# Attention, Fourier mixing and an MLP: the last batch's q and k in natural order, and the last row tile's second matrix in two halves

## The chip, the cores and the metric

The kernel runs on one core of one Trainium2 chip. The metric is the device time of one launch in microseconds (us), lower is better. Five engines work from queues of their own: TensorE (PE in the profile, with its weight loads as PEld), VectorE (DVE), ScalarE (ACT), GpSimd (POOL), and SyncE (SP), which here only issues transfers.

## The reference, cut to what matters

```python
# q, k, v: (4, 8, 768, 64); mem_k, mem_v: (4, 8, 8, 64)
for c in range(768 // 32):                    # chunks of 32 queries
    k_full = concat(mem_k, k[16 left of the chunk : 8 right of it])
    v_full = concat(mem_v, v[the same rows])
    out[chunk] = softmax(q[chunk] @ k_full.T / 8) @ v_full
x = out with the heads side by side           # (4, 768, 512)
u = x + real(fft(fft(x, axis=1), axis=2))
un = (u - mean(u)) / sqrt(var(u) + 1e-6)
y = u + relu(un @ w_ch1) @ w_ch2              # 512 -> 2048 -> 512
```

## The kernel before, in words

There are four batches (b = 0 to 3), and each goes through three stages: attention, a Fourier transform by matrices, and the MLP. Attention works on pairs of heads, four pairs to a batch, numbered n = 0 to 15; a pair fills the 128 partitions with 2 x 64 head dimensions. For each pair, q and k are loaded (`e_load_qk`, cast to bf16 by the GpSimd queue), turned so that the head dimension lies on the partitions, and k is spread into twelve windows of 128 columns, `kTb`: 32 zeros, 8 memory keys, and 88 keys (16 left, 64 own, 8 right) for every 64 queries (`e_kT`). Then come two groups (g = 0, 1) of scores (`e_scores`, 12 matmuls of 64 columns each), the exponential on ACT (`e_exp`), the values (`e_values`, 24 matmuls) and the division (`e_norm`, DVE).

A load puts 8 rows of q or k side by side on one partition (row = 8 p + j, RB = 8), so the turned matrix has its columns in the order j, then p. In batches 0 to 2 TensorE turns them (`turn`), and the copies out of PSUM (`e_qT`, `e_kT`, line 415) put the columns back in natural order. In batch 3 (`b >= TURNED`) a transposing DMA on SP does the turning (`e_flip_q`, `e_flip_k`), and the order stays interleaved: `e_kT` (line 410, on ACT) gathers each window with a stride of 128 columns, and `e_scores` reads q in runs of 8 and writes its 64 scores with a stride of 8, so that they come out in natural order. `kU`, the turned k of batch 3 with a margin of zeros, is cleared once at the start by GpSimd (line 851).

The MLP takes three row tiles at a time (sh = 0, 1). `e_ch1` (line 741) makes 16 blocks of 128 hidden units by 384 rows, 4 matmuls each; `e_relu` (ACT, line 749) moves each to SBUF; then for each row tile `e_ch2` (line 756) adds 16 matmuls of 512 columns in one PSUM bank, `e_osb` (DVE, line 763) multiplies by the row's scale and adds u, and a store follows. Four PSUM banks serve the MLP and the Fourier stage (`acc0`, `acc1`, `mlp0`, `mlp1`). In batches 1 to 3 row tiles 3 to 5 are stored in two hops (lines 771 and 778: the Fourier stage leaves their rows mirrored); the others in one (`e_out`, line 768). The order of the row tiles in these batches is 0, 3, 4, 5, 1, 2, so the last tile of all is 2, stored in one hop from ACT's queue.

The order on every engine is fixed beforehand by `Plan.order`, a scheduler in Python: each task (`add`) has an engine, a cost in us, what it comes after, and the buffers that it takes and gives back. On every engine the first task in rank order that can start by the plan's clock is put next. MLP matmuls have a very high rank number (`MLPS`) and are marked `filler=True`: they fill whatever TensorE time the earlier stages leave. The costs that the plan uses are estimates; the chip then executes each engine's list in order, whatever the times turn out to be.

Of the kernel before, what the change touches and what calls it, by code (L numbers as in the profile page):

```python
# [177 lines left out]
def kernel(  # L178
# [54 lines left out]
        assert False  # L233

    NS = 3
    qs = [spool.tile([QP, 2, RB * D], BF16, name=f"qs{i}") for i in range(NS)]
    ks = [spool.tile([KP, 2, RB * D], BF16, name=f"ks{i}") for i in range(NS)]
    NV = 4
    va = [spool.tile([P, 2, NT, 66], FP32, name=f"va{i}") for i in range(NV)]
    NKT = 2  # L240
    KR, KS, NKU = 16, 128, 2
    kU = [spool.tile([P, RB, KS], BF16, name=f"kU{i}") for i in range(NKU)]
    kTb = [spool.tile([P, NT, P], BF16, name=f"kTb{i}") for i in range(NKT)]

    TURNED = 3
# [92 lines left out]
    def e_load_qk(n, i):  # L338
        b, pr = seq[n]
        src, dst = ((q, qs), (k, ks))[i]  # L340
        if b >= TURNED:
            for hh in range(2):
                nc.gpsimd.dma_start(
                    dst[n % NS][0:QP].rearrange("p h (j d) -> p (h j) d", d=D)[:, hh::2],
                    src[b, 2 * pr + hh].rearrange("(p j) d -> p j d", j=RB))
            return
        nc.gpsimd.dma_start(dst[n % NS][0:QP],  # L347
                            src[b, 2 * pr:2 * pr + 2].rearrange("h (p j) d -> p h (j d)", j=RB))
# [21 lines left out]
    def turn(out_, src, eye):  # L370
        w = eye.shape[1]
        for j in range(RB):
            for hh in range(2):
                nc.tensor.transpose(out_[64 * hh:64 * hh + 64, j * w:(j + 1) * w],  # L374
                                    src[:, hh, j * D:(j + 1) * D], eye)

    def e_flip_q(n):
        qT_of[n] = qT = apool.tile([P, RB, QP], BF16, tag="qT", bufs=2, name="qT")
        nc.sync.dma_start_transpose(qT, qs[n % NS].rearrange("p h c -> p (h c)"))

    def e_flip_k(n):
        nc.sync.dma_start_transpose(kU[n % NKU][:, :, KR:KR + QP],
                                    ks[n % NS][0:QP].rearrange("p h c -> p (h c)"))

    def e_turn_q(n):
        tr_of[n] = trq = aps.tile([P, S], BF16, tag="tr", bufs=1, name="trq")
        turn(trq, qs[n % NS], ident_b[0:QP, 0:QP])

    def e_qT(n):
        qT_of[n] = qT = apool.tile([P, S], BF16, tag="qT", bufs=2, name="qT")  # L390
# [3 lines left out]
    def e_turn_k(n):  # L394
        if n < HP:
            trk = bank("acc", [P, RB * KP], BF16, "trk")
        else:
            trk = aps.tile([P, RB * KP], BF16, tag="tr", bufs=1, name="trk")
        tr_of[n, 1] = trk
        turn(trk, ks[n % NS], turn_b)  # L400

    def e_mkT(n):
        b, pr = seq[n]
# [3 lines left out]

    def e_kT(n, eng=None):
        if n >= TURNED * HP:
            nc.scalar.copy(  # L410
                strided(kTb[n % NKT], MEM0 + NMEM, [[P, NT], [RB, 11], [1, RB]]),
                strided(kU[n % NKU], KR - KOFF, [[64 // RB, NT], [1, 11], [KS, RB]]))
            return
        trk = tr_of.pop((n, 1))
        (eng or nc.scalar.copy)(
            strided(kTb[n % NKT], MEM0 + NMEM, [[P, NT], [RB, 11], [1, RB]]),
            strided(trk, 0, [[64 // RB, NT], [1, 11], [KP, RB]]))
        if n < HP:
            let_go(trk)

    def e_scores(n, g):
        qT, kT = qT_of[n], kTb[n % NKT]
        sc_of[n, g] = sc = aps.tile([P, 2, 8, 64], FP32, tag="sc", bufs=1, name="sc")
        for t6 in range(6):
            t = 6 * g + t6
            for hh in range(2):
                r0 = 64 * hh
                if n < TURNED * HP:
                    own, to = qT[r0:r0 + 64, ts(t, 64)], sc[:, hh, t6, :]
                else:  # L430
                    own = strided(qT[r0:r0 + 64], t * 64 // RB, [[QP, RB], [1, 64 // RB]])
                    to = strided(sc[:, hh, t6, :], 0, [[1, RB], [RB, 64 // RB]])
                nc.tensor.matmul(to, kT[r0:r0 + 64, t, :], own, start=True, stop=True,  # L433
                                 tile_position=(r0, 0))

    def e_exp(n, g):
# [291 lines left out]
    def slot(b, i):  # L728
        return SLOT[i] if b else i
# [22 lines left out]
    def e_ch2(b, sh, stl, part):  # L752
        if part == 0:
            pc_of[b, sh, stl] = bank(pick(b, sh, stl, 0)["tag"], [P, DM], FP32, "pc")
        for ht in range(4 * part, 4 * part + 4):
            nc.tensor.matmul(pc_of[b, sh, stl], hT_of[b, sh][:, ht, ts(stl, P)], w2_sb[:, ht, :],  # L756
                             start=(ht == 0), stop=(ht == NHT - 1))

    def e_osb(b, sh, stl):
        st = slot(b, sh * 3 + stl)  # L760
        osb_of[b, st] = osb = fpool.tile([P, DM], FP32, tag="osb", bufs=4, name="osb")
        pc = pc_of.pop((b, sh, stl))
        nc.vector.scalar_tensor_tensor(osb, pc, rstd_of[b][:, st:st + 1], xs[b][:, st, :],  # L763
                                       ALU.mult, ALU.add)
        let_go(pc)
# [87 lines left out]
    def attention(n):  # L853
        nonlocal t_gate
        b, pr = seq[n]
        first = b == 0
        lq, lk = [add("POOL", 1.6 if b >= TURNED else 0.9, lambda i=i: e_load_qk(n, i),
                      take=(("qs", "ks")[i],), moved=3.1 if b >= TURNED else 1.2, grain=0.032 if b >= TURNED else 0.1, late=LATE if b else 0.0,
                      behind=t_gate if n == HP else t_xr[b - 2] if n == TURNED * HP else t_ck.get(n - 1),
                      rank={0: -4 + i, 1: -1.2 + 0.1 * i, 2: 10 + 0.1 * i}.get(n)) for i in range(2)]  # L860
        lv = add("SP", 2.5, lambda: e_load_v(n), [t_ones[n] if n < NV else None],
                 behind=t_x2.get(b - 2),
                 take=("va",), moved=2.6, grain=0.031, head=0.4, late=(0.0, 4.0, LATE, LATE)[b])
        t_lv[n] = lv
        t_ck[n] = lk
        if n == HP - 1:
            def e_gate():
                nc.gpsimd.tensor_copy(gate[64:65], va[n % NV][64:65, 1, NT - 1, 0:1])

            t_gate = add("POOL", 0.1, e_gate, [lv])  # L870
        mk = t_mk[n] = add("DVE", 0.2, lambda: e_mkT(n), [t_mkT, t_kTz[n % NKT], t_mk.get(n - 1)],
                           take=("kTb",))
        if b >= TURNED:
            eq = add("SP", 1.2, lambda: e_flip_q(n), [lq], take=("qT",), give=("qs",),
                     late=5.0, loose=True, behind=t_flip[0])
            t_flip[0] = tk = add("SP", 1.2, lambda: e_flip_k(n), [lk, t_uz], take=("kU",),
                                 give=("ks",), late=5.0, loose=True, behind=eq)
            ek = add("ACT", 2.05, lambda: e_kT(n), [tk, mk], give=("kU",))
        else:
            tq = add("PE", 0.40, lambda: e_turn_q(n), [lq, t_idb], take=("tr",), give=("qs",))  # L880
            dve = ("DVE", nc.vector.tensor_copy) if n < HP else ("ACT", None)
            eq = add("ACT", 0.80, lambda: e_qT(n), [tq], take=("qT",), give=("tr",),
                     rank=SINES - 0.5 if n == 0 else None)
            ktag = "acc" if first else "tr"
            tk = add("PE", 0.43, lambda: e_turn_k(n), [lk, t_idb, t_kz if n == 0 else t_kzs],
                     take=(ktag,), give=("ks",))
            ek = add(dve[0], 1.25 if dve[1] else 1.04, lambda: e_kT(n, dve[1]), [tk, mk],
                     give=(ktag,))
        for g in range(2):
            s_ = add("PE", 0.32, lambda g=g: e_scores(n, g), [eq, ek], take=("sc",),  # L890
                     give=("qT", "kTb") if g == 1 else ())
            t_sc[n, g] = s_
            t_exp[n, g] = x_ = add("ACT", 1.12, lambda g=g: e_exp(n, g),
                     [s_, t_masks, t_after.get(n)], take=("e1",), give=("sc",))
            tag = "mlp" if first and g == 1 else "xa"
            v_ = add("PE", 0.85, lambda g=g: e_values(n, g), [x_, lv, t_low[n % NV]], take=(tag,),
                     rank=len(plan.tasks) + (50 if (n, g) == (2, 1) else 25) if first else None,
                     give=("e1", "va") if g == 1 else ("e1",))
            take = ("xsb",) if g == 0 and n % HP == 0 else ()
            t_norm[n, g] = add("DVE", 0.78, lambda g=g: e_norm(n, g),  # L900
                               [v_, t_norm[n - n % HP, 0] if (n % HP, g) != (0, 0) else None],
                               take=take,
                               give=(tag,))
        return x_
# [198 lines left out]
    def mlp(b, t_un, rs):  # L1103
        for sh in range(2):
# [10 lines left out]
                                rank=RELU(len(plan.tasks))))  # L1115
            for stl in range(3):
                st, end_b = slot(b, 3 * sh + stl), 3 * sh + stl == NST - 1
                for part in range(4):
                    end = part == 3
                    c2 = add("PE", 0.88, lambda sh=sh, stl=stl, part=part: e_ch2(b, sh, stl, part),  # L1120
# [68 lines left out]
```

The softmax here doesn't subtract the row's maximum and nothing guards it: scores larger than these inputs give would overflow.

## Time and profile before

The time is 290.89 us (290.84 to 291.22, 3 runs); the profiled execution spans 289.2 us, at a granted TensorE clock of 0.999.

| | PE | PEld | DVE | ACT | POOL |
|---|---|---|---|---|---|
| busy, us | 272.9 | 170.5 | 166.0 | 167.7 | 65.1 |
| share of the span | 94% | 59% | 57% | 58% | 23% |

| group | count | mean ns |
|---|---|---|
| first matrix, 128x384 (L741) | 512 | 326 |
| second matrix, 128x512 (L756) | 384 | 380 |
| sum and scale of one row tile, DVE (L763) | 24 | 751 |
| scores (L433) | 384 | 205 |
| spread of k, ACT, batch 3 (L410) | 4 | 2059 |
| spread of k, ACT, batches 1 and 2 (L415) | 8 | 1038 |

Matmuls overlap in the pipeline, so a mean duration is not the time that one takes from its neighbour; that is read from the starts, and the chain of waits gives it. The chain is followed back from the last instruction: at each step to what released it. The windows give the busy time of each engine in a stretch of the span.

### The profile page before, as it was taken

To read this page: it belongs to the slowest core of one execution; us is meant where nothing else is said; L and a number is where in the kernel's file an instruction comes from. 1 tells how busy PE (TensorE), PEld (TensorE's weight loads), DVE (VectorE), ACT (ScalarE), POOL (GpSimd) and SP (SyncE) were. 2 spreads that over 40 slices of the span, in tenths; PEclk is the share of its full clock that TensorE was granted. 3 is DMA by queue.
4 is the path that set the end of the run, shared out by engine and by line. 5 is a ranking of instruction groups with operands and counts; after the bars stand their busy time and mean duration, and the time that the engine had idled before them with its cause. 6 is when DMAs were issued, how large, how long until landed. Compare 5 with 4: busy or idle time off the path is not lost.

```text
span 289.2 us, 7127 instructions
## 1 busy us (share of the span) xinstructions
PE 272.9 (94%) x2932; PEld 170.5 (59%) x2932; DVE 166.0 (57%) x345; ACT 167.7 (58%) x290; POOL 65.1 (23%) x115
## 2 busy tenths in 40 slices
PE   1588989999999999999999999999999999999994
PEld 1466678866665767556676656556654544645641
DVE  7967998862239876958675984985672012012011
ACT  6887446688777587836796466526660721712700
POOL 8844893330210172441001002010020000000000
PEclk9999999999999999999999999999999999999999
DMA  6998989999999999999797047784142504004204
GB/s 110 198 174 150 199 159 206 199 201 195 198 190 257 130 223 166 138 152 220 177 173 176 27 111 145 175 141 159 20 89 85 100 9 125 14 36 105 42 36 109
DMA packets 115968, 39.92 MB, mean 138 GB/s; under 512 B 104544, under 2 KB 111200, under 8 KB 115936
## 3 DMA queue, kind: packets, MB, share of 16 engines
q1 hardware_dynamic: 93744, 23.41, 44.8%
q0 software_dynamic: 21472, 15.21, 32.5%
q10 hardware_dynamic: 720, 0.85, 0.9%
q8 instruction: 23, 0.38, 0.5%
q14 instruction: 9, 0.07, 0.1%
HBM read 37.36 MB, written 13.37 MB: 175 GB/s over the span
## 4 chain that ended last, share of the span: by engine, by line
PE 85%; DVE 6%; POOL 5%; DMA 2%; issue 2%; ACT 0%; POOLq 0%
PE pc L756 29%; PE ph L741 29%; PE xa L456 7%; PE ps L528 5%; PE pm L679 5%; PE sc L433 3%; DMA ks<-in_k_dram 2%; PE trk L374 1%; DVE ff L615 1%; PE trq L374 1%; POOL qs L347 1%; DVE hl L635 1%; DVE up L545 1%; DVE xsb L467 1%; PE pm L579 1%
## 5 line engine op out<-in xcount | busy, mean ns | idle before, releaser
L749 ACT ACTIVATE hT<-ph 128x384 f16<-128x384 f32 x128 | 61.9, 491 | 50.6 <-PE ph L741 49.8
L741 PE MATMUL ph<-unT,w_sb 128*128 128x384 f16 x512 | 88.1, 326 | 0.0
L756 PE MATMUL pc<-w_sb,hT 128*128 128x512 f16 x384 | 87.8, 380 | 0.0
L741 PEld LDWEIGHTS <-w_sb 128*128 128x128 f16 x512 | 48.6, 98 | 32.0 <-issue 0.4
L756 PEld LDWEIGHTS <-hT 128*128 128x128 f16 x384 | 35.9, 98 | 41.0 <-issue 0.4
L763 DVE SCALAR_TENSOR_TENSOR osb<-pc,rstd,xsb 128x512 f32<-128x512 f32 x24 | 18.0, 751 | 69.3 <-PE pc L756 64.8
L440 ACT ACTIVATE e<-sc,mbias 128x384 f32<-128x384 f32 x64 | 33.6, 577 | 18.8 <-PE sc L433 18.8
L456 PEld LDWEIGHTS xa<-va,e 128*64 128x64 f32 x672 | 21.9, 137 | 7.2 <-issue 6.2
L456 PE MATMUL xa<-va,e 128*64 128x65 f32 x672 | 25.8, 226 | 0.0
L699 ACT ACTIVATE un<-xsb,mu_s 128x512 f16<-128x512 f32 x24 | 16.9, 719 | 6.6 <-DVE mu_s L694 6.6
L540 ACT CAST up<-ps 128x386 f16<-128x386 f32 x16 | 9.6, 602 | 13.8 <-PE ps L528 11.6
L693 DVE BATCH_NORM_STATS2 st<-xsb 128x6 f32<-128x512 f32 x24 | 16.6, 691 | 0.7
L467 DVE TENSOR_TENSOR xsb<-xa,zs 128x384 f32<-128x384 f32 x28 | 15.6, 558 | 1.0
L466 DVE RECIPROCAL zs<-xa 128x6 f32<-128x6 f32 x28 | 5.3, 190 | 18.1 <-PE xa L456 17.7
L518 DVE TENSOR_TENSOR lo<-ff,hi 128x768 f16<-128x768 f32 x12 | 11.4, 954 | 4.7 <-ACT hi L513 4.7
L545 DVE TENSOR_TENSOR up<-ps,up 128x386 f16<-128x386 f32 x16 | 9.5, 596 | 6.9 <-ACT up L540 6.7
L433 PE MATMUL sc<-qT,kTb 64*128 64x64 bf16 x384 | 12.6, 205 | 0.5 <-ACT e L440 0.5
L433 PEld LDWEIGHTS <-kTb 64*128 64x128 bf16 x384 | 8.5, 100 | 7.3 <-issue 6.1
L571 POOL DMA_DIRECT2D xr<-x_back x3 | 2.3, 778 | 44.3 <-DMA x_back<-x_rows 44.3
L513 ACT CAST hi<-ff 128x768 f16<-128x768 f32 x12 | 9.9, 827 | 3.3 <-DVE ff L505 3.0
L374 PE MATMUL trq<-ident_b,qs 96*64 96x96 bf16 x192 | 7.0, 220 | 5.1 <-DMA qs<-in_q_dram 5.1
L685 DVE TENSOR_TENSOR xsb<-pm,xsb 128x512 f32<-128x512 f32 x15 | 10.0, 672 | 3.2 <-PE pm L679 3.2
(150 smaller groups left out, 356.9 us busy)
## 6 DMA issues: line engine op xcount, KB each, us to landing
va<-in_v_dram SPq DMA_DIRECT2D x32, 220.0 KB
w_sb<-in_moe_w_ch_dram POOLq DMA_DIRECT2D x8, 512.0 KB, 15.1
out_dram<-osb SPq DMA_DIRECT2D x12, 256.0 KB
qs<-in_q_dram POOLq DMA_DIRECT2D x12, 192.0 KB, 6.2
ks<-in_k_dram POOLq DMA_DIRECT2D x12, 192.0 KB, 6.9
x_rows<-xsb POOLq DMA_DIRECT2D x3, 768.0 KB, 5.1
xr<-x_back POOLq DMA_DIRECT2D x3, 768.0 KB, 6.5
out_rows<-osb SPq DMA_DIRECT2D x9, 256.0 KB
```

The costliest lines, as they stand in the source:

```text
L433: nc.tensor.matmul(to, kT[r0:r0 + 64, t, :], own, start=True, stop=True, tile_position=(r0, 0))
L440: nc.scalar.activation(e1[:, :, :, ts(half, 32)], sc[:, :, 0:6, ts(half, 32)], AFT.Exp, bias=mbias[:, half:half + 1], scale=1.0 / math.sqr ...
L456: nc.tensor.matmul(xa[64 * half:64 * half + 64, st, hh, 0:65], e1[:, hh, t6, :], v1[:, hh, 6 * g + t6, 0:65], start=True, stop=True)
L467: nc.vector.tensor_tensor(xs[b][:, 3 * g:3 * g + 3, 2 * pr * D:(2 * pr + 2) * D] .rearrange("p s (h d) -> p s h d", h=2), xa[:, :, :, 0:D] ...
L528: nc.tensor.matmul(out_[:, sp, :], part[:, ab, sp * 3 + st, c0:c1], tab[:, sp, st, :], start=(st == 0 and i == 0), stop=(st == 2 and i == 1))
L679: nc.tensor.matmul(pm[:, par, :], lhs, rhs[:, par, :], start=(im == 0), stop=(im == 3))
L693: nc.vector.bn_stats(st6, xs[b][:, kt, :])
L699: nc.scalar.activation(un, xs[b][:, kt, :], AFT.Identity, bias=mu_of[b][:, kt, 0:1], scale=-1.0)
L741: nc.tensor.matmul(ph[:, 0:384], w1_sb[:, dt, ts(ht, P)], unT_of[b][:, dt, sh * 384:(sh + 1) * 384], start=(dt == 0), stop=(dt == NDT - 1))
L749: nc.scalar.activation(hT_of[b, sh][:, ht, :], ph[:, 0:384], AFT.Relu, bias=0.0, scale=-1.0)
L756: nc.tensor.matmul(pc_of[b, sh, stl], hT_of[b, sh][:, ht, ts(stl, P)], w2_sb[:, ht, :], start=(ht == 0), stop=(ht == NHT - 1))
L763: nc.vector.scalar_tensor_tensor(osb, pc, rstd_of[b][:, st:st + 1], xs[b][:, st, :], ALU.mult, ALU.add)
```

## The change

It has two parts. In batch 3 the loads put row p of each block of 128 on partition p, so that the transposing DMA leaves q and k in natural order. Scores then read and write runs of 64 as in the other batches, and the spread of k copies runs of 88 keys, which is given to DVE in place of ACT. `kU` shrinks from 1024 to 800 columns. In the last row tile of the last batch the second matrix is done as two halves of 256 columns, each with its own PSUM bank, its own sum on DVE and its own store (the first from SP, the second from ACT), so that the work after the last matmul is half as large.

```diff
-    qs = [spool.tile([QP, 2, RB * D], BF16, name=f"qs{i}") for i in range(NS)]
-    ks = [spool.tile([KP, 2, RB * D], BF16, name=f"ks{i}") for i in range(NS)]
+    qs = [spool.tile([P, 2, RB * D], BF16, name=f"qs{i}") for i in range(NS)]
+    ks = [spool.tile([P, 2, RB * D], BF16, name=f"ks{i}") for i in range(NS)]
...
-    KR, KS, NKU = 16, 128, 2
-    kU = [spool.tile([P, RB, KS], BF16, name=f"kU{i}") for i in range(NKU)]
+    KR, NKU = 16, 2
+    kU = [spool.tile([P, KR + S + KR], BF16, name=f"kU{i}") for i in range(NKU)]
...
-                    dst[n % NS][0:QP].rearrange("p h (j d) -> p (h j) d", d=D)[:, hh::2],
-                    src[b, 2 * pr + hh].rearrange("(p j) d -> p j d", j=RB))
+                    strided(dst[n % NS], hh * D, [[2 * D, NST], [1, D]]),
+                    src[b, 2 * pr + hh].rearrange("(a p) d -> p a d", p=P))
...
-        nc.sync.dma_start_transpose(qT, qs[n % NS].rearrange("p h c -> p (h c)"))
+        nc.sync.dma_start_transpose(qT.rearrange("p (a s) -> p a s", s=P),
+                                    qs[n % NS].rearrange("p h c -> p (h c)")[:, 0:S])
...
-        nc.sync.dma_start_transpose(kU[n % NKU][:, :, KR:KR + QP],
-                                    ks[n % NS][0:QP].rearrange("p h c -> p (h c)"))
+        nc.sync.dma_start_transpose(kU[n % NKU][:, KR:KR + S].rearrange("p (a s) -> p a s", s=P),
+                                    ks[n % NS].rearrange("p h c -> p (h c)")[:, 0:S])
...
         if n >= TURNED * HP:
-            nc.scalar.copy(
-                strided(kTb[n % NKT], MEM0 + NMEM, [[P, NT], [RB, 11], [1, RB]]),
-                strided(kU[n % NKU], KR - KOFF, [[64 // RB, NT], [1, 11], [KS, RB]]))
+            win = LEFT + 64 + RIGHT
+            nc.vector.tensor_copy(
+                strided(kTb[n % NKT], MEM0 + NMEM, [[P, NT], [1, win]]),
+                strided(kU[n % NKU], KR - LEFT, [[64, NT], [1, win]]))
...
-                if n < TURNED * HP:
-                    own, to = qT[r0:r0 + 64, ts(t, 64)], sc[:, hh, t6, :]
-                else:
-                    own = strided(qT[r0:r0 + 64], t * 64 // RB, [[QP, RB], [1, 64 // RB]])
-                    to = strided(sc[:, hh, t6, :], 0, [[1, RB], [RB, 64 // RB]])
-                nc.tensor.matmul(to, kT[r0:r0 + 64, t, :], own, start=True, stop=True,
+                nc.tensor.matmul(sc[:, hh, t6, :], kT[r0:r0 + 64, t, :],
+                                 qT[r0:r0 + 64, ts(t, 64)], start=True, stop=True,
                                  tile_position=(r0, 0))
...
+    def e_ch2_half(b, sh, stl, half):
+        pc_of[b, sh, stl, half] = pc = bank(pick(b, sh, stl, 1 + half)["tag"], [P, HD], FP32, "pc")
+        for ht in range(NHT):
+            nc.tensor.matmul(pc, hT_of[b, sh][:, ht, ts(stl, P)], w2_sb[:, ht, ts(half, HD)],
+                             start=(ht == 0), stop=(ht == NHT - 1))
+
+    def e_osb_half(b, sh, stl, half):
...
+        nc.vector.scalar_tensor_tensor(osb, pc, rstd_of[b][:, st:st + 1], xs[b][:, st, cols],
+                                       ALU.mult, ALU.add)
...
+    def e_out_half(b, st, half):
+        (nc.sync, nc.scalar)[half].dma_start(out[b, ts(st, P), ts(half, HD)],
+                                             osb_of.pop((b, st, half)))
...
-            ek = add("ACT", 2.05, lambda: e_kT(n), [tk, mk], give=("kU",))
+            ek = add("DVE", 0.6, lambda: e_kT(n), [tk, mk], give=("kU",))
...
+                if end_b and b == B - 1:
+                    for half in range(2):
+                        c2 = add("PE", 1.76, lambda sh=sh, stl=stl, half=half:
+                                 e_ch2_half(b, sh, stl, half), [relu[-1], t_w2[3], c2],
+                                 pick=pick(b, sh, stl, 1 + half), rank=MLPS + len(plan.tasks))
+                        os_ = add("DVE", 0.4, lambda sh=sh, stl=stl, half=half:
+                                  e_osb_half(b, sh, stl, half), [c2, rs], take=("osb",),
+                                  give=(pick(b, sh, stl, 1 + half),))
+                        add(("SP", "ACT")[half], 0.5, lambda st=st, half=half:
+                            e_out_half(b, st, half), [os_], give=("osb",), moved=0.5)
+                    continue
```

## The prediction

> **What bounds the kernel now.** I read the page first (shares of engines), then the windows, the chain of waits in order of time, the answers for the tiles concerned, and last the DMA share at the end. The page gives TensorE 94% of the span:
>
> ```profile
> PE 272.9 (94%) x2932; PEld 170.5 (59%) x2932; DVE 166.0 (57%) x345; ACT 167.7 (58%) x290; POOL 65.1 (23%) x115
> ```
>
> The windows say where the missing 6% lies: of 10 us each, TensorE is busy for 10.00 in every stretch from 50 us to 280 us, and the gaps are all at the start and after the last matmul. The list of waits from 50 to 286 us has none for TensorE. The columns here are the stretch, its length, and the busy us of PE, PEld, DVE, ACT and POOL, then clock and DMA.
>
> ```profile
> 20.00:30.00 10.00, 8.79 (x206) 6.46 (x204) 7.41 (x18) 7.21 (x12) 4.48 (x7) 1.00 0.94 166
> 50.00:60.00 10.00, 10.00 (x184) 7.53 (x183) 9.06 (x22) 7.63 (x14) 2.54 (x4) 1.00 1.18 202
> 130.00:140.00 10.00, 10.00 (x142) 6.36 (x142) 8.43 (x15) 7.12 (x13) 0.78 (x1) 1.00 1.27 245
> 160.00:170.00 10.00, 10.00 (x121) 6.46 (x120) 9.40 (x21) 5.01 (x9) 0.00 (x0) 1.00 0.22 56
> 280.00:289.20 9.20, 5.21 (x25) 2.16 (x22) 1.50 (x2) 0.00 (x0) 0.00 (x0) 0.97 0.41 112
> ```
>
> So the time is a start of about 50 us, a block of TensorE work without a hole, and a tail. A microsecond of TensorE work removed from the block should come off the end; one removed from another engine should not. The chain in order of time (start, us, what) shows the two kinds of score groups, both with 12 matmuls of 64 columns, and the tail:
>
> ```profile
> 117.81 0.87 PE pm L679 x8
> 118.68 0.28 PE sc L433 x12
> ...
> 131.71 0.44 PE sc L433 x12
> ...
> 274.85 10.37 PE pc L756 x48
> 285.25 0.75 DVE osb L763
> ```
>
> 0.28 us is a group of batch 2 or earlier, 0.44 one of batch 3. In the chain there are eight of 0.44 (131.71, 134.21, 139.81, 151.26, 154.39, 156.81, 164.61, 167.63), all groups of batch 3. The tail: the last matmul ends at 285.22, DVE takes 0.75, ACT issues the store at 286.03, its bytes move from 286.8 to 287.6 by the DMA share in slices of 0.2 us, and the span ends at 289.2.
>
> Two more answers matter: the copies of the tile kTb (ns min/median/max), and the chain near 15 us, which passes through the clearing of kU.
>
> ```profile
> L410 ACT COPY kTb<-kU x4: 2047/2054/2080, 125.9 to 158.9; 128x1056 bf16<-128x1056 bf16 x4
> L404 DVE COPY kTb<-mkT x16: 177/184/980, 11.2 to 155.9; 128x96 bf16<-128x96 bf16 x16
> ```
>
> ```profile
> 15.13 0.52 POOL kU L851
> ...
> 16.07 0.95 POOL kU L851
> 17.02 0.58 POOL qs L347
> 17.60 5.32 DMA ks<-in_k_dram
> ...
> 22.97 0.55 PE trk L374 x16
> ```
>
> **What the Trainium skill says.** "Advanced Engine Details and Errata", PSUM Cachelines: PSUM lines are 8 bytes, and any pattern that isn't contiguous slows matmuls significantly. The trace agrees: the groups that write with a stride of 8 take 0.44 / 12 = 37 ns a matmul, the contiguous ones 0.28 / 12 = 23 ns. "TensorE: Matmul & The Clock Gate", Back-to-back issue gap: N / 2.4 + 2.5 ns. It fits: 10.37 / 48 = 216 ns at 512 columns, and 0.87 / 8 = 109 ns at 256 (pm, above), so halves cost almost no more than wholes. "VectorE: DVE Perf Modes", The perf-mode tier table: a 16-bit copy from SBUF to SBUF goes at up to four elements a cycle, fp32 out of PSUM at one. "DMA: Bandwidth & Descriptors", Anatomy of one DMA: a transfer costs some 2.0 us fixed, mostly the receipt of the write, plus bytes / 436 GB/s; here 1.6 us pass from the last byte at 287.6 to the end.
>
> **The change part by part.**
>
> *Scores in natural order (the block).* Eight groups go from 0.44 to 0.28, since instruction and operands become those of batches 0 to 2: 8 x 0.16 = 1.28 us less TensorE work. The bounds are narrow, as both forms are in the trace: 1.2 to 1.35.
>
> *Spread of k from ACT to DVE (off the path).* ACT loses 4 x 2.05 = 8.2 us. The DVE copy of 1056 elements isn't in the trace. From the 96-element copy (184 ns, about 0.16 of it fixed) at 4 elements a cycle it is 0.16 + 1056 / 4 / 960 MHz = 0.43 us; at two elements a cycle 0.71. I take 0.45: DVE gets 1.8 us more (to 2.8) between 125 and 160 us, where it is 63 to 84% busy. It costs nothing: TensorE has MLP matmuls of earlier batches in hand; the last matmuls of batch 3's Fourier stage end near 211 us, and its MLP starts at 243.7 (285.25 less four blocks of 10.4), so batch 3 may come 30 us late.
>
> *A wait that changes engine.* The copy of k waits for the transposing DMA. Before, that stopped ACT (1.5 us once, for kU); now it stops DVE, and behind it in DVE's queue stand sums that free PSUM banks (L763), divisions (L467) and the Fourier copies. TensorE waits for these only when all four banks are held. I take 0, because TensorE did not stop when ACT, which frees the banks of the first matrix, stood 1.5 us; the other end is the slow rival below.
>
> *Loads and flips.* 768 pieces of 256 bytes for each head either way (96 x 8 or 128 x 6), and the same bytes turned. They run beside the block: 0.
>
> *Clearing kU (the start).* Two GpSimd memsets of 1024 columns take 0.97 us each; 384 columns (L820) take 0.42, so 0.86 ns a column and 800 columns take 0.78: 2 x 0.19 = 0.39 us less. They stand in front of the issue of pair 3's loads, on the chain, so those are issued 0.39 earlier. The transfer of 5.32 us runs among loads of v, and may or may not land that much earlier. I take 0.25 (0 to 0.4).
>
> *The tail.* Halves: 32 x 109 = 3.49 against 16 x 216 = 3.46, +0.04 (up to 0.15 if the change of bank opens a gap). DVE on 256 columns: 751 less 256 / 960 MHz = 0.48 us, so -0.27. The store has half the bytes: its 0.8 us of movement becomes 0.4 at best; by the price (131 KB less at 436 GB/s) 0.30 less. I take -0.30 (0 to 0.4). The first half's sum and store begin 1.75 us before the last matmul ends, and its bytes are through before the second store is issued. Sum of the tail: -0.53.
>
> *Order of the plan.* A different engine and cost for the copy changes the planned order after 125 us. A group put behind another kind of work can cost TensorE 0.1 more (two ch2 parts take 1.73 or 1.83 in the chain). Five more or five fewer such places are 0.5 us either way; I take 0.
>
> Total: -1.28 - 0.25 - 0.53 = -2.06, so 290.89 - 2.06 = 288.8 us (0.7% less).
>
> **The rivals.**
>
> 1. *The new order takes back half.* If the altered plan has ten more seams at 0.1 us, or the start gives nothing and a few short waits appear, about 1 us is lost: 289.9. For it: five engines are ordered from estimated costs. Against: the total work is the same, so seams should fall as often as they rise. 0.18.
> 2. *DVE becomes the holder of the banks: slower.* DVE is 84% busy at 130 to 140 us and 94% at 160 to 170. If each of the four copies stood 1.5 us (the wait ACT had) for its flip and TensorE lost it all, that is 6.0 - 2.06 = +3.9, 294.8; with half of it, 291.8. Against: no wait of TensorE in the whole block. 0.06.
> 3. *No change that can be measured:* the middle of these, gains of 2 us met by a loss of about as much; 290.3 to 291.5. 0.05.
> 4. *More than forecast:* the start gives its full 0.4, fewer seams save 0.4: 288.2 or less. 0.08.
>
> **How the numbers follow.** The likeliest case has 0.63: 288.3 to 289.5, with its centre at 288.8. I stretch the range to 288.1 to cover most of case 4, and to 290.0 for most of rival 1; what stays out is some 0.05 below and 0.13 above. Faster by over 0.2% (under 290.31): 0.63 + 0.08 + 0.18 = 0.89; within 0.2%: 0.05; slower: 0.06.
>
> **What would show it right or wrong.** Right: eight batch-3 score groups at 0.28 in the chain; TensorE still at 10.00 in every window from 50 us on; the last matmul 1.5 us or so earlier than 285.22; the last DVE sum near 0.48; from its end to the end of the span about 2.9 us in place of 3.2; kU's memsets near 0.78 and pair 3's turn of k before 22.97. Wrong: PE waiting on DVE (the sum, L763) after 125 us, windows below 10.00 there, a DVE copy of k that takes over 1 us, or a tail that ends no sooner because the store's time doesn't follow its bytes.

## The result, and the profile after

The changed kernel takes 289.31 us (288.94 to 289.51, 5 runs) against 291.22 us for the kernel before in the same runs (290.84 to 292.13). The ratio is 0.993, with a 95% interval of 0.991 to 0.995: 1.9 us less by the medians. The profiled execution spans 287.6 us against 289.2.

The windows of the kernel after (stretch, length, busy us of PE, PEld, DVE, ACT and POOL, clock, DMA):

```profile
50.00:60.00 10.00, 10.00 (x185) 7.54 (x183) 9.06 (x22) 7.63 (x14) 2.55 (x4) 1.00 1.17 201
130.00:140.00 10.00, 10.00 (x127) 6.34 (x126) 8.45 (x16) 6.70 (x14) 0.76 (x1) 1.00 1.30 223
160.00:170.00 10.00, 10.00 (x78) 5.39 (x76) 9.56 (x23) 7.01 (x13) 1.17 (x2) 1.00 0.39 92
280.00:287.60 7.60, 4.20 (x36) 3.23 (x33) 1.72 (x3) 0.00 (x0) 0.00 (x0) 0.94 0.42 104
```

TensorE is still busy for all of every 10 us from 50 us on; its list of waits from 50 us to the last matmul is empty, as before. So the change must show as a shorter block, an earlier start of the block, or a shorter tail. In the views, ph is the first matrix of the MLP, pc the second, sc the scores, xa the values, trk the turn of k, tp the turn of the normalized rows, and pm and ps belong to the Fourier stage. The chain of waits in order of time (start, us, what), kernel after:

```profile
57.81 1.41 PE ph L739 x8
...
118.70 0.28 PE sc L430 x12
...
131.15 0.28 PE sc L430 x12
...
273.80 6.91 PE pc L754 x32
280.70 3.51 PE pc L760 x32
284.24 0.48 DVE osb L767
```

The score group at 131.15 belongs to batch 3 and now takes 0.28 like that of batch 2 at 118.70. All eight do. The 32 matmuls of 256 columns take 3.51, against 3.46 for 16 of 512. The last matmul ends at 284.21 (285.22 before), the last sum takes 0.48 (0.75 before), and from the last matmul to the end of the span there are 3.39 us (3.98 before).

From here on I measure the block as the time from the first MLP group (first `ph` of the chain) to the end of the last matmul. In the profile before the first `ph` starts at 57.79, and in the profile after at 57.81. The block is then 285.22 - 57.79 = 227.43 before and 284.21 - 57.81 = 226.40 after. So 1.03 came from the block, 0.59 from the tail, and nothing from the start: together 1.6 us, which is the difference of the two spans, and lies within the interval of the times.

The spread of k on DVE and the clearing of kU, from the answers for the tiles kTb and kU, kernel after:

```profile
L412 DVE COPY kTb<-kU x4: 425/426/608, 127.1 to 169.2; 128x1056 bf16<-128x1056 bf16 x4
```

```profile
L867 POOL MEMSET kU<- x2: 770/772/775, 15.0 to 15.7; 128x800 bf16 x2
```

Both costs are as worked out (0.43 and 0.78). Two of the terms of the sum are not: the start gave nothing, though the memsets did shrink, and the block shrank by 1.03, where eight score groups alone should give 1.28 and the halves take back only 0.04 to 0.05.

### The profile page after: what moved, and what is told of

It reads as the page before. It is cut to its first block, busy times and chain, and to the rows that moved or that the text cites. A ratio compares the mean times of both kernels' runs of the same rounds, so it can differ in the third digit from the quotient of the medians.

```text
span 287.6 us, 7167 instructions
## 1 busy us (share of the span) xinstructions
PE 272.2 (95%) x2948; PEld 171.2 (60%) x2948; DVE 169.2 (59%) x350; ACT 160.5 (56%) x286; POOL 65.4 (23%) x115
## 4 chain that ended last, share of the span: by engine, by line
PE 86%; POOL 5%; DVE 4%; DMA 2%; issue 2%; POOLq 0%
PE ph L739 30%; PE pc L754 28%; PE xa L454 7%; PE ps L526 5%; PE pm L677 5%; PE sc L430 3%; DMA ks<-in_k_dram 2%; PE ps L666 2%; PE trk L374 1%; DVE ff L613 1%; PE pc L760 1%; PE trq L374 1%; POOL qs L347 1%; DVE hl L633 1%; DVE xsb L465 1%
## 5 line engine op out<-in xcount | busy, mean ns | idle before, releaser
L754 PE MATMUL pc<-w_sb,hT 128*128 128x512 f16 x368 | 84.4, 380 | 0.0
L754 PEld LDWEIGHTS <-hT 128*128 128x128 f16 x368 | 34.3, 98 | 38.7 <-issue 0.2
L779 DVE SCALAR_TENSOR_TENSOR osb<-pc,rstd,xsb 128x512 f32<-128x512 f32 x23 | 17.2, 749 | 63.5 <-PE pc L754 60.9
L691 DVE BATCH_NORM_STATS2 st<-xsb 128x6 f32<-128x512 f32 x24 | 16.6, 691 | 0.7
L430 PEld LDWEIGHTS <-kTb 64*128 64x128 bf16 x384 | 7.7, 95 | 7.3 <-issue 5.9
L430 PE MATMUL sc<-qT,kTb 64*128 64x64 bf16 x384 | 11.3, 193 | 0.5 <-ACT e L438 0.5
L392 ACT COPY qT<-trq 128x768 bf16<-128x768 bf16 x12 | 9.5, 795 | 3.5 <-PE trq L374 3.5
```

Of the source, the lines that this page charges most:

```text
L430: nc.tensor.matmul(sc[:, hh, t6, :], kT[r0:r0 + 64, t, :], qT[r0:r0 + 64, ts(t, 64)], start=True, stop=True, tile_position=(r0, 0))
L691: nc.vector.bn_stats(st6, xs[b][:, kt, :])
```

## The experiments

My theory after reading the two traces: natural order is worth 1.28 exactly; the other plan adds two seams (a seam is a place where TensorE goes from an attention group to MLP or Fourier work, called wide work below, and back), which cost 0.1 each; the halves cost TensorE 0.04 and shorten the tail; and the start has a second path that absorbs the shorter memsets. The rivals are in the expectations. This is what all twelve runs gave. The ratio is to the kernel before on the same chip; flat_write and flat_read were timed once each and have none. The first four columns come from one profiled execution of each kernel.

| run | first ph | last matmul ends | block | from there to the end | time, us | ratio (95%) |
|---|---|---|---|---|---|---|
| before | 57.79 | 285.22 | 227.43 | 3.98 | | |
| after | 57.81 | 284.21 | 226.40 | 3.39 | 289.31 | 0.993 (0.991 to 0.995) |
| natural_same_plan | 58.19 | 284.33 | 226.14 | 3.97 | 289.97 | 0.9963 (0.9949 to 0.9977) |
| natural_same_plan_dve | 57.15 | 283.29 | 226.14 | 4.01 | 289.78 | 0.9955 (0.9938 to 0.9972) |
| natural_only | 60.41 | 286.77 | 226.36 | 3.93 | 290.02 | 0.9970 (0.9959 to 0.9982) |
| halves_only | 57.68 | 285.15 | 227.47 | 3.45 | 290.63 | 0.9984 (0.9975 to 0.9992) |
| same_plan_halves | 58.35 | 284.53 | 226.18 | 3.37 | 289.41 | 0.9930 (0.9907 to 0.9952) |
| same_plan_384_128 | 58.28 | 284.47 | 226.19 | 3.13 | 289.21 | 0.9918 (0.9889 to 0.9947) |
| flat_write | 58.29 | 284.44 | 226.15 | 3.96 | 290.17 | timed once |
| flat_read | 57.82 | 285.25 | 227.43 | 3.95 | 290.95 | timed once |
| kU_short | 57.21 | 284.70 | 227.49 | 4.00 | 291.15 | 0.9993 (0.9981 to 1.0006) |
| kU_double | 59.23 | 286.65 | 227.42 | 3.95 | 292.42 | 1.0047 (1.0031 to 1.0063) |
| kU_short_no_gate | 57.30 | 284.73 | 227.43 | 3.97 | 291.03 | 0.9997 (0.9982 to 1.0011) |
| coarse_fill | 57.99 | 290.94 | 232.95 | 3.56 | 296.84 | 1.0194 (1.0169 to 1.0219) |

The first two columns show why the block is the measure here. It repeats to 0.07 us between kernels with the same TensorE work (227.42 to 227.49 in five of them), while the start of one profiled execution varies by microseconds: natural_only's profile begins its MLP 2.6 us later than the kernel before, though the work up to there is that of the kernel after. (In that execution score groups took 0.43 us up to 20 us and 0.28 only from 23 us on; in the kernel before they took 0.28 from 16.6 us on.)

### Natural order with the plan's order unchanged

```diff
-            ek = add("DVE", 0.6, lambda: e_kT(n), [tk, mk], give=("kU",))
+            ek = add("ACT", 2.05, lambda: e_kT(n), [tk, mk], give=("kU",))
...
-            nc.vector.tensor_copy(
+            nc.scalar.copy(
                 strided(kTb[n % NKT], MEM0 + NMEM, [[P, NT], [1, win]]),
...
-                if end_b and b == B - 1:
+                if False:
```

This is against the kernel after. The plan sees the old engine and cost, so TensorE's list is in the same order as before, matmul for matmul.

> Natural order alone, without the halves, with the copy of k left on ACT and planned at its old cost of 2.05 us: TensorE's list then has the same order as in the kernel before. Theory (TensorE's block is the bound, a score group costs 0.28 in place of 0.44, each extra seam 0.1, the start gives nothing): eight groups, no extra seam, so the last matmul ends 1.28 us earlier than in the kernel before (285.22 becomes 283.94) and the time falls by 1.3 us. Rival (the start's shorter clearing does arrive, 0.25 to 0.4, and the block loses more elsewhere): 1.5 to 1.7 us less, and the first MLP group begins before 57.5. Rival (natural order itself gives only 1.06, as in the changed kernel): 1.06 less.

The chain of natural_same_plan, at the two ends of the block and at the first score group of batch 3:

```profile
58.19 1.41 PE ph L739 x8
...
132.10 0.28 PE sc L430 x12
...
282.80 1.52 PE pc L754 x7
284.33 0.03 issue
```

The block is 226.14, which is 1.29 under before, against 8 x 0.16 = 1.28. The instant named in the expectation (283.94) was not met, as the block began 0.4 later in this execution; its length is what the theory says. The instants named for the next two were missed in the same way (283.29 and 286.77), and there too the length of the block decides.

> As natural_same_plan, with the copy of k executed by DVE at the place in the plan where ACT had it; TensorE's order is still that of before. Theory (the 0.2 us missing from the block in the changed kernel is the planned order): the same as natural_same_plan, last matmul at 283.9 to 284.0. Rival (the copy on DVE, or its wait for the flip, costs the 0.2): 0.2 later, 284.15, and TensorE waits for DVE show in the block.

```diff
-            nc.scalar.copy(
+            nc.vector.tensor_copy(
                 strided(kTb[n % NKT], MEM0 + NMEM, [[P, NT], [1, win]]),
```

(against natural_same_plan). The block is 226.14 again, and TensorE has no wait in it. The copy of k on DVE, with its wait for the transposing DMA (the flip), costs TensorE nothing. This takes away the rival for the missing 0.2.

> The first part of the change as it is (copy on DVE, planned at 0.6), without the halves. Theory: scores -1.28, two more seams after attention groups +0.2: last matmul 1.06 earlier (284.15), time 1.1 us less. Rival (natural order is worth the full 1.28 here too, and the halves cost 0.2 of the block): 283.95.

natural_only is the kernel after without the branch for the halves (`if False:` as above). Its block is 226.36: 0.22 more than with the old order. The difference between this run and natural_same_plan_dve is only where the plan puts things. (By the times, 0.9970 against 0.9955, the two can't be told apart.) In the order of TensorE's list the step from an attention group to wide work comes 46 times before and 48 times after; in the block alone, 38 and 40 times. The chain of the kernel after shows such a place, and one within wide work:

```profile
63.61 0.65 PE ph L739 x4
...
171.14 0.76 PE ph L739 x4
171.90 0.28 PE sc L430 x12
```

Four matmuls of 384 columns take 0.65 between other wide work and 0.76 between two attention groups. The starts of the matmuls say where the 0.1 lies. These are the last of the four and what follows it, first within wide work, then in front of scores (timeline of the kernel after):

```profile
63.93 0.33 PE L739 MATMUL ph<-unT,w_sb 128*128 128x384 f16 x1
64.09 0.28 PE L704 MATMUL tp<-ident_h,un 128*128 128x128 f16 x2
```

```profile
171.57 0.33 PE L739 MATMUL ph<-unT,w_sb 128*128 128x384 f16 x1
171.83 0.26 PE L430 MATMUL sc<-qT,kTb 64*128 64x64 bf16 x6
```

The step back from wide work to attention takes 0.26 in place of 0.16. Each of the 38 steps back in the block of natural_same_plan_dve takes 0.09 to 0.10 longer than the usual step within wide work, 3.56 us in all; the 40 of natural_only take 3.76. That is 0.20 of the 0.22. The step out of attention adds nothing of its own: from the last matmul of the values 0.15 pass until the next one starts, whether that is the MLP's or that of another score group. Why the step back takes longer is not shown.

### The halves alone

```diff
+                if end_b and b == B - 1:
+                    for half in range(2):
+                        c2 = add("PE", 1.76, lambda sh=sh, stl=stl, half=half:
+                                 e_ch2_half(b, sh, stl, half), [relu[-1], t_w2[3], c2],
...
```

(the second part of the change, on the kernel before)

> The second part alone on the kernel before: last row tile's second matrix, sum and store in two halves. Theory: last matmul 0.04 later (285.27), DVE's last sum 0.48 in place of 0.75, store 2.85 in place of 3.17 us from issue to the end: span and time 0.54 us less. Rival (a store's time is fixed, its size doesn't matter): 0.23 less. Rival (the first half's store delays the second): no gain.

From the timeline of halves_only (start, us, engine, line):

```profile
283.43 0.48 DVE L769 SCALAR_TENSOR_TENSOR osb<-pc,rstd,xsb 128x256 f32<-128x256 f32 x1 [0.99 <-PE pc L762]
283.94 0.34 SPq L774 DMA_DIRECT2D out_dram<-osb  x1
285.17 0.48 DVE L769 SCALAR_TENSOR_TENSOR osb<-pc,rstd,xsb 128x256 f32<-128x256 f32 x1 [1.26 <-PE pc L762]
285.69 0.34 ACTq L774 DMA_DIRECT2D out_dram<-osb  x1
```

The first half is summed and handed to SP while TensorE does the second. The block grows by 0.04; after the last matmul 3.45 us remain in place of 3.98. The sum gives 0.27 of that. The store gives the rest: from issue to the end 288.6 - 285.69 = 2.91 here, 2.85 in the kernel after, and 3.17 before. Neither rival holds: a store of half the size does end sooner, by about 0.3, and no delay by the first can be seen. The time is 0.5 us under before; its interval, 0.2 to 0.7, just touches the first rival's 0.23, so it is the traces that decide.

### Which stride costs

The change makes both the read of q and the write of the scores contiguous. Two kernels do one each.

```diff
-                    to = strided(sc[:, hh, t6, :], 0, [[1, RB], [RB, 64 // RB]])
+                    to = sc[:, hh, t6, :]
```

> The kernel before, with batch 3's scores written in one run of 64 (they come out in interleaved order, so batch 3's result is not the reference's) while q is still read in eight runs of 8. Theory (the stride of 8 in PSUM is the price[...]): a group takes 0.28 to 0.30 and the block shrinks by 1.1 to 1.3 us. Rival (the reads in short runs are the price): groups stay near 0.44.

```diff
-                    own = strided(qT[r0:r0 + 64], t * 64 // RB, [[QP, RB], [1, 64 // RB]])
+                    own = qT[r0:r0 + 64].rearrange("p j s -> p (j s)")[:, ts(t, 64)]
```

> The kernel before, with batch 3's q read in one run of 64 of its interleaved columns (so the queries of a window are the wrong ones and batch 3's result is not the reference's) while the scores are still written with a stride of 8. Theory (the stride in PSUM is the price): groups stay at 0.42 to 0.44, the block within 0.15 us of before. Rival (the reads): 0.28 to 0.30 and 1.1 to 1.3 us off the block.

The first score group of batch 3 in the chain, flat_write and then flat_read:

```profile
132.22 0.28 PE sc L433 x12
```

```profile
131.74 0.44 PE sc L433 x12
```

The whole 0.16 lies in the write with a stride of 8 fp32 into PSUM. (The matmuls of a group start in pairs, one for each head; from the second pair on, the next one follows after 29 ns in flat_write and after 56 ns in flat_read.) The read in runs of 8 bf16 costs nothing: flat_read's block is 227.43, the kernel before's to the hundredth, and flat_write's is 226.15, that of the full natural order.

### The start

```diff
-    t_uz = add("POOL", 0.4, lambda: [nc.gpsimd.memset(kU[i], 0.0) for i in range(NKU)], rank=20)
+    t_uz = add("POOL", 0.4, lambda: [nc.gpsimd.memset(kU[i][:, :, s:s + 16], 0.0)
+                              for i in range(NKU) for s in (0, KR + QP)], rank=20)
```

> The kernel before, with only the margins of kU cleared by GpSimd (4 memsets of 128 columns, some 0.8 us together, in place of 2 of 1024 columns and 1.95 us), so pair 3's loads are issued about 1.1 us earlier. Theory (a second path of nearly the same length, pair 3's v landing at 25.5 and GpSimd's work behind it that holds DVE until 29.5, absorbs it): the first MLP group begins as in the other runs (57.2 to 58.2), time the same within 0.2 us. Rival (the chain as the profile drew it, through kU, the loads and the turn of k, has no slack behind it): 0.7 to 1.1 us faster.

Pair 3's k is issued at 16.39 in place of 17.60, yet the time is the same (0.9981 to 1.0006, so at most 0.55 us of a gain of 1.1 can be there). This one profile begins its block 0.58 earlier than that of the kernel before, but the 22 times do not follow it (291.15 against 291.22). The chain of kU_short shows what stands behind:

```profile
8.65 7.78 DMA ks<-in_k_dram
16.43 0.14 issue
16.57 0.54 PE trk L374 x16
...
17.44 1.05 ACT e L440 x2
18.49 0.92 ACT va L329
...
22.88 0.35 PE trk L374 x15
```

It no longer goes through GpSimd. It goes through pair 2's k, which arrives at 16.43, and then through ACT's exponentials and TensorE's list of the earlier pairs, and so to pair 3's turn. (The chain counts a matmul from the end of the one before it, 22.88 here. By the starts this turn begins at 22.66, and in the kernel before at 22.97.) Two things took most of the 1.21 us. Pair 3's k, issued that much earlier, landed only 0.52 earlier (22.40 against 22.92): its transfer took 6.0 us in place of 5.3, and over the traces of this case it takes between 4.8 and 6.3. And TensorE, which had waited for it before, came to the turn only 0.26 after the landing. That leaves 0.3.

> The kernel before, with each kU cleared twice: 1.95 us more on GpSimd in front of pair 3's loads. Theory (absorbed one way, but the slack of the second path is short, about 0.5 us or less in this direction): 1.4 to 2.0 us slower. Rival (the loads are bound by the transfers alone, and the issue time does not matter in either direction): the same within 0.2 us.

With `for i in (0, 1, 0, 1)` in that memset, 1.4 us are lost of the 1.95 added. So the path does count in one direction: lengthening it shows, and no gain from shortening it can be seen.

> As kU_short, and GpSimd's gate no longer waits for pair 3's v (it writes a constant, so batch 1's first loads are issued earlier and run beside that v). Theory (the gate is the second path): 0.3 to 0.8 us faster than the kernel before, GpSimd's fold (zy) begins before 26.3. Rival (the transfers themselves are the limit; batch 1's loads now take their share from pair 3's v): no gain or slower, pair 3's values start later.

```diff
-                nc.gpsimd.tensor_copy(gate[64:65], va[n % NV][64:65, 1, NT - 1, 0:1])
+                nc.gpsimd.memset(gate[64:65], 0.0)
```

This was on top of kU_short. The gate is a copy of one element on GpSimd that holds back batch 1's loads until pair 3's v is there. My guess that it is the second path fell: without this wait no gain can be seen, and GpSimd then waits for DVE's division instead. In this trace pair 3's k landed at 21.21, and TensorE still came to its turn only at 22.81, 1.6 later. That supports the path which kU_short's chain shows; no kernel here shortens that path by itself.

In the profile after, the turn did come earlier (22.46 against 22.97), and the half microsecond was lost a little later. The timelines there, kernel before and then kernel after (zy and ff are sums of batch 0 in front of its Fourier stage):

```profile
26.68 1.96 POOL L596 TENSOR_TENSOR zy<-xsb 128x384 f32<-128x384 f32 x2
27.77 0.90 DVE L610 COPY ff<-zy 128x3 f32<-128x3 f32 x1
28.58 1.02 DVE L615 TENSOR_TENSOR ff<-zy,xsb 128x381 f32<-128x381 f32 x2
```

```profile
26.86 2.33 POOL L594 TENSOR_TENSOR zy<-xsb 128x384 f32<-128x384 f32 x2
27.26 0.62 DVE L608 COPY ff<-zy 128x3 f32<-128x3 f32 x1
27.79 1.81 DVE L613 TENSOR_TENSOR ff<-zy,xsb 128x381 f32<-128x381 f32 x2
```

DVE comes to these sums half a microsecond earlier, and both kernels end them at 29.60. GpSimd's two sums run at the same time. In the kernel before, DVE's small copy takes 0.90 and ends at 28.67, 0.02 after GpSimd's sums; where GpSimd's sums are over it takes 0.16 (same_plan_384_128). In the kernel after, the second of the two L613 takes 1.33 in place of 0.54. The Trainium skill, "SBUF — State Buffer", Who interferes with whom, says that a DVE instruction with two SBUF inputs contends with a GpSimd instruction that reads SBUF. It fits, as L613 has two such inputs, and three more traces have an L613 of 1.34 beside GpSimd's second sum (natural_same_plan_dve, same_plan_halves and coarse_fill). I ran no kernel that takes GpSimd's work away there, so that this is what ate the gain is argued and not shown.

### The two parts with the old order, and a smaller last piece

> Natural order with ACT's copy at its old planned cost (TensorE's order as before) and the two halves. Theory: the parts add: block 1.29 less and 0.04 more, tail 0.53 less after the last matmul: 227.43 becomes 226.18 from the first MLP group to the last matmul, time 1.8 us under before, 0.2 under the changed kernel. Rival (halves and order interact, as the plan has a gap at the end): no better than the changed kernel, 226.40.

same_plan_halves is the kernel after with natural_same_plan's two edits for ACT's copy. The parts add as expected: block 226.18, then 3.37 us. By the trace that is 0.24 under the kernel after (0.22 in the block); by the times (0.9930 against 0.993) the two can't be told apart.

> same_plan_halves with the last row tile cut into 384 and 128 columns in place of 256 and 256. Theory (after the last matmul come a sum that goes by its columns and a store that goes by its bytes; a matmul of 128 columns takes 0.22 / 4 = 55 ns, as in the turns tp): TensorE 16 x (162 + 55) = 3.48, as before; the last sum 0.35 in place of 0.48; the store about 0.15 shorter; from the last matmul to the end 3.1 us in place of 3.39, time 2.1 us under the kernel before. Rival (weight loads of 98 ns bound the short matmuls: 16 x 98 = 1.57 in place of 0.88): 0.7 later on TensorE and no gain. Rival (the first store, now three quarters of the tile, is still moving when the last is issued): the last store takes as long as with halves, 2.85.

```diff
+    CUT = ((0, 384), (384, 128))
...
-            nc.tensor.matmul(pc, hT_of[b, sh][:, ht, ts(stl, P)], w2_sb[:, ht, ts(half, HD)],
+            nc.tensor.matmul(pc, hT_of[b, sh][:, ht, ts(stl, P)], w2_sb[:, ht, ds(*CUT[half])],
```

The end of same_plan_384_128 in the timeline:

```profile
283.60 0.62 DVE L769 SCALAR_TENSOR_TENSOR osb<-pc,rstd,xsb 128x384 f32<-128x384 f32 x1 [1.85 <-DMA out_dram<-out_rows]
284.24 0.34 SPq L774 DMA_DIRECT2D out_dram<-osb  x1
284.49 0.35 DVE L769 SCALAR_TENSOR_TENSOR osb<-pc,rstd,xsb 128x128 f32<-128x128 f32 x1 [0.28 <-PE pc L762]
284.88 0.34 ACTq L774 DMA_DIRECT2D out_dram<-osb  x1
```

The block stays (226.19), so short matmuls are not held by their weight loads here. The last sum is 0.35, and the last store takes 287.6 - 284.88 = 2.72. From the last matmul to the end: 3.13. In the trace this is the shortest of all, 0.47 us under the kernel after; its time of 289.21 us (0.9889 to 0.9947) is within the uncertainty of it.

### Fewer seams

> same_plan_halves with the second matrix of a row tile planned as one piece of 16 matmuls in place of four of 4: TensorE's order then enters MLP or Fourier work from an attention group 39 times in place of 46. Theory (each such seam costs 0.1 us): 0.6 to 0.8 us less TensorE time than same_plan_halves if TensorE still never waits; time about 2.5 us under before. Rival (pieces of 3.5 us delay attention and the Fourier stage so much that TensorE runs out of work, or the start gets longer): no gain over same_plan_halves or slower, with TensorE below 10.00 in some window after 50.

```diff
-                for part in range(4):
+                for part in range(1):
...
-                    c2 = add("PE", 0.88, lambda sh=sh, stl=stl, part=part: e_ch2(b, sh, stl, part),
+                    c2 = add("PE", 3.52, lambda sh=sh, stl=stl, part=part: e_ch2(b, sh, stl, part),
```

(against same_plan_halves, with the 16 matmuls in one piece). It is 1.9% slower. The chain of coarse_fill:

```profile
123.53 3.56 PE pc L754 x16
127.09 0.87 PE pm L677 x8
127.97 0.30 PE sc L430 x12
...
129.62 5.05 DMA unT<-un
134.67 0.14 issue
134.81 1.44 PE ph L739 x4
```

TensorE runs out of work. Batch 0's MLP is used up before batch 1's normalized rows have been turned by the DMA, so TensorE stands for 5 us, and the first group after the hole is slow (1.44 against 0.65); the granted clock of the stretch from 130 to 140 us was 0.66. The rival of the expectation holds. The part about the seams holds too: the block of this trace has 31 steps back to attention in place of 38, and 30 of them take 0.09 to 0.10 longer than the usual step within wide work (one, in the slow stretch, takes 0.29 longer). Seven fewer are worth some 0.7, and the hole costs far more. The absence of waits in the kernel before hangs on when the plan spends its filler.

## Why the prediction was right, and where it was not

The time predicted, 288.8 us, was 2.06 under the 290.89 of the kernel before; measured were 289.31, and 1.9 under the kernel before in the same runs. By its steps:

- **What bounds the kernel.** Right. A microsecond of TensorE work in the block came off the end (natural_same_plan: 1.29 removed from the block, 1.16 by the medians), and moving the copies of k from ACT (4 x 1.08) to DVE gave nothing by itself (226.14 in both runs).
- **Scores in natural order, -1.28.** Right to 0.01 us, and the cause named (the stride into PSUM, not the reads) is shown by flat_write and flat_read.
- **Order of the plan, 0.** This term was mis-sized: +0.22. I had the price of a seam right (0.1) and the number of extra ones at 0; there were 2. I had put the price on the group behind another kind of work; it falls on the step back to attention.
- **Clearing kU, -0.25.** This step failed: it gave 0, the low end of its range. The memsets shrank by 0.4 as worked out, and pair 3's turn came earlier in the profile after, but nothing of it reached the block. I took the gain from the chain of waits, which shows only the path that ended last. kU_short and kU_short_no_gate show another path close behind it; which of the things found there absorbs the gain is not shown.
- **The tail, -0.53.** Right: -0.59 after the last matmul, +0.04 in front of it. Sum and store each gave what was worked out. The price of a transfer that the prediction cites is given for transfers issued by GpSimd, and this store goes from ACT's queue. Its rate came out (0.30 worked out for the bytes, 0.26 to 0.34 measured). Its fixed 2.0 us did not: 3.17 us less 0.60 for 256 KB at that rate leave 2.57, an estimate.
- **Copy of k on DVE, wait for the flip, loads, flips: 0.** Right (natural_same_plan_dve has the same block as natural_same_plan). The copy takes 0.43 where I had taken 0.45.

With the two steps as measured the sum is -1.29 + 0.22 + 0 - 0.55 = -1.62. That is what the spans say (289.2 to 287.6). The medians of the times say -1.9, which lies nearer to the predicted -2.06 than the measured parts do; the interval of the ratio, -1.5 to -2.6 us, covers both, and the start varies by this much from one execution to the next. So part of the closeness to 2.06 is chance.

## What to carry to other kernels

Where one engine has no hole for most of the span, price a change by what it takes from that engine's own list, and compare traces by the length of that block and not by the span; the start can vary by more than the change is worth. The chain of waits says what a longer step would cost, not what a shorter one would bring: look for the second path before you book a gain. And where a planner fixes the order, a changed cost reshuffles it; count the seams, and watch that the filler lasts until the next stage is ready.

## What the runs showed of the hardware

- A group of 12 bf16 matmuls of 64 columns, which start two at a time, takes 0.28 us when each writes a run of fp32 in PSUM and 0.44 with a stride of 8 (flat_write and flat_read): a pair every 29 ns or every 56 ns. Reading the moving operand in runs of 8 bf16 adds nothing.
- Going back from MLP or Fourier matmuls to an attention group costs TensorE 0.09 to 0.10 us each time, with no wait shown (0.26 against 0.16 after a matmul of 384 columns).
- The same 1056 elements of k on each partition take 2.05 us on ACT when gathered with a stride of 128 columns (before), 1.08 on ACT in runs of 88 (natural_same_plan) and 0.43 on DVE in runs of 88 (after).
- A DVE sum of 128 x 381 fp32 with two SBUF inputs takes 0.54 us, and 1.33 where it runs beside a GpSimd sum (after).
- The last store takes 3.17 us from issue to the end of the span at 256 KB, 2.83 to 2.91 at 128 KB, and 2.72 at 64 KB (before; halves_only, same_plan_halves and after; same_plan_384_128): most of it does not depend on the size.
- The sum on DVE takes 0.75, 0.62, 0.48 and 0.35 us at 512, 384, 256 and 128 columns, which is a fixed 0.22 and 1.04 ns a column.
